# A 32x32 matrix per head, loaded into four groups of partitions: one transfer with a leading stride of 0, or four transfers

## The chip, the cores and the metric

The kernel runs on one core of a Trainium2 chip. The metric is the time of one execution on the device in microseconds, as the median of several runs. TensorE is written PE (its weight loads PEld), VectorE DVE, ScalarE ACT, GpSimd POOL; SP issues all transfers of this kernel.

## The reference

A recurrent attention block and a gated feed-forward block behind it:

```python
# r, k, v, w, a, b: (B, H, S, D) = (4, 8, 768, 40)
for t in range(S):
    y[:, :, t] = einsum('bhd,bhde->bhe', rt, state)
    Sa = einsum('bhde,bhe->bhd', state, at)
    state = state * wt[:, :, None, :] - einsum('bhd,bhe->bhde', Sa, bt)
    state = state + einsum('bhd,bhe->bhde', vt, kt)
x = y.transpose(0, 2, 1, 3).reshape(B * S, H * D)          # 3072 x 320
xn = x / sqrt(mean(x * x) + 1e-6) * rms_g
out = (silu(xn @ w_gate) * (xn @ w_val)) @ w_out           # 320 -> 1536 -> 320
```

The inputs arrive in double precision and are narrowed to fp32 in the kernel for the weights.

## The kernel before, in words

The 768 steps are cut into 24 chunks of 32. Within a chunk the recurrence is solved with matrices, for all 32 pairs of batch and head at once. Each chunk passes three functions:

- `front(c)` loads the tokens (`wan`, `kbn`, `VU`), turns them on TensorE and builds, over five levels, the 32x32 triangular matrix of each pair in the tile `LT`. At its end the lower half of `LT` is written to a buffer in memory, `sB` (32 pairs by 1024 numbers, two transfers), and from there it is loaded into the tile `M` (128 partitions by 32 by 32). `M` holds the 32 matrices four times, once in each group of 32 partitions. There is one `M` buffer.
- `inverse(c)` inverts them by substitution on VectorE, in 31 steps of two operations (`tmp<-Yi,M` and `Yi<-Yi,tmp`). Each group of 32 partitions does 8 of the 32 rows of the inverse (`Yi`), which is why each needs its own copy of `M`. The result goes through the buffer `sY` (four transfers) back into `LT` (two transfers).
- `main(c)` uses the inverse and the state `ST`, computes the outputs `y` of the chunk over the levels (`psC`), turns and normalises them (`ss`, `x`) and puts them into `xg`.

After every second chunk, `feed(g)` runs the feed-forward block on 256 rows: six pairs of weight tiles `wf` (five buffers, loaded again from `sW` each time), into `psH`, `sg`, `hT` and `psO`. Before the first chunk is done, `narrow` prepares the weights in `sW`.

No engine's order is written out by hand. Every operation is added to a `Plan` with its engine, a due time, a cost and its operands. `Plan.issue` then plays the engines in its own time: whichever engine is free takes, of the operations whose inputs it holds to be ready, the one with the earliest due time. The program is issued in that order, and each engine executes its own part strictly in order. The price of a transfer is a term of the plan (line 216 on): 0.06 on the queue, and its result is held to be ready 2.2 us and the bytes at 200 GB/s later, plus 0.1:

```python
    def dma(due, o, i, by="SP"):
        q, t = {"SP": (nc.sync, 0.06), "POOL": (nc.gpsimd, 1.0)}[by]
        n = size(i) * list(i.ap)[0][1]
        plan.add(by, due, t, lambda: q.dma_start(out=o, in_=i), [o], [i], 2.2 + n * 4 / 200e3)
```

`n` counts the elements of the source's access pattern, repeats included. The due time of the transfers at the end of `front(c)` is `(c - 2) * T + T - 8`, that of the inverse steps `(c - 1) * T + 4 + i`, with `T = 46`.

In the profile the helpers' lines stand for whole classes of operations: L183 is any two-operand VectorE operation, L195 the masked copy into `LT`, L219 any transfer, L222 any matmul, L225 any turn. So rows are told apart by the names of their tiles.

Of the kernel before, what the change touches and what calls it, by code (L numbers as in the profile page):

```python
# [17 lines left out]
C = 32  # L18
# [89 lines left out]
def kernel(  # L108
# [42 lines left out]
    BH = B * H  # L151
# [17 lines left out]
    def side(t, l, x):  # L169

        return t.rearrange("p n (g x l) -> p n g x l", x=2, l=l)[:, :, :, x, :]
# [4 lines left out]
    def size(ap):  # L176
        n = 1
        for _, m in list(ap.ap)[1:]:
            n *= m
        return n  # L180

    def tt(due, o, a, b, op):
        plan.add("DVE", due, 0.145 + 0.00104 * size(o), lambda: nc.vector.tensor_tensor(o, a, b, op), [o], [a, b])  # L183
# [10 lines left out]
    def where(due, o, m, a):  # L194
        plan.add("DVE", due, 0.16 + 0.00104 * size(o), lambda: nc.vector.copy_predicated(o, m, a), [o], [m, a, o])  # L195

    def copy(due, o, a):
        plan.add("ACT", due, 0.16 + 0.00083 * size(o), lambda: nc.scalar.copy(o, a), [o], [a])  # L198
# [11 lines left out]
    def ptt(due, o, a, b, op):  # L210
        plan.add("POOL", due, 0.2 + 0.0021 * size(o), lambda: nc.gpsimd.tensor_tensor(o, a, b, op), [o], [a, b])  # L211

    def pcopy(due, o, a):
        plan.add("POOL", due, 0.15 + 0.0014 * size(o), lambda: nc.gpsimd.tensor_copy(o, a), [o], [a])
# [6 lines that stand above are left out]
    def mm(o, lhsT, rhs, start=True, stop=True):  # L221
        return o, lhsT, rhs, lambda: nc.tensor.matmul(o, lhsT, rhs, start=start, stop=stop, skip_group_check=True)  # L222
# [4 lines left out]
    def pe(due, time, steps):  # L227
        def issue():
            for s in steps:
                s[3]()  # L230
        plan.add("PE", due, time, issue, [s[0] for s in steps], [x for s in steps for x in s[1:3]])
# [19 lines left out]
    for p0, kt, src in ((0, 0, 0), (0, 1, P), (0, 2, 2 * P), (64, 2, 2 * P)):  # L251
        m = min(P, DM - src)
# [64 lines left out]
    def turned(due, t, tag):  # L317

        ps = ps_[tag].next().rearrange("p u f -> p (u f)").rearrange("p (n t) -> p n t", n=N)
        pe(due, 0.95, [flip(ps[:, n, :], t[:, n].rearrange("p o e -> p (o e)"), ident) for n in range(N)])  # L320
        return ps

    def tokens(due, t, i, x, src, tk):
        dma(due, flat(t)[rows(i, x), :, 0:D], src[2 * i:2 * i + 2, :, tk, :].rearrange("q h s d -> s (q h) d"))

    def natural(due, l, K):
        ps = turned(due, K.rearrange("p (n i) x s -> p n i (x s)", i=2), "B")
        t = KN_[l].next()
        copy(due, t[:, 0:NI * D].rearrange("p (n o e) -> p n o e", n=N, o=2),
             ps.rearrange("p n (o e) -> p n o e", o=2)[:, :, :, 0:D])  # L330
        return t
# [5 lines left out]
    def front(c):  # L337

        z = Z[c] = {}
        d = (c - 2) * T  # L340
        tk = slice(c * C, (c + 1) * C)
        wa, kb, z["VU"] = wan.next(), kbn.next(), VU_.next()
        for i in range(2):
            tokens(d - T, wa, i, 0, w, tk)
            tokens(d - T, wa, i, 1, a, tk)
            tokens(d - T, kb, i, 0, k, tk)
            tokens(d - T, kb, i, 1, b, tk)
            tokens(d - T, z["VU"], i, 0, v, tk)
        ps = turned(d, wa, "B").rearrange("p n (i x t) -> p (n i) x t", i=2, x=2)
        Tt = T_.next()  # L350
        z["T"] = Tl = {}
        o = 0
        for l in LEVELS + (32,):
            Tl[l] = Tt[:, o:o + NI * C // l].rearrange("p (n t) -> p n t", n=NI)
            o += NI * C // l
        copy(d, Tl[1], ps[:, :, 0, :])
        A = A_.next()
        copy(d, A, ps[:, :, 1, :])
        K = K_.next()
        copy(d + 2, K.rearrange("p (n i) x s -> p n (i x s)", n=N), turned(d + 2, kb, "B"))  # L360
        LT = z["LT"] = LT_.next()
        z["KN"] = {1: flat(kb).rearrange("p a e -> p (a e)")}
        for j, l in enumerate(LEVELS):
            G = C // (2 * l)
            due = d + 5 + 7.5 * j
            gr = ps_["B"].next().rearrange("p o (n t) -> p o n t", n=N)[:, :, :, 0:16]
            pe(due, 0.95, [mm(gr[half(i), o, n, :], K[part(o), 2 * n + i].rearrange("p x s -> p (x s)"),
                              side(A, l, 1)[part(o), 2 * n + i]) for n, i, o in each])
            where(due, side(LT, l, 1), side(msk, l, 1)[:, j:j + 1].bitcast(U32).to_broadcast((P, NI, G, l)),
                  gr.rearrange("p o n t -> p (o n) t").rearrange("p n (g l) -> p n g l", g=G))  # L370
            if l > 1:
                z["KN"][l] = natural(due + 2, l, K)

            t = Tl[l].rearrange("p n (g x) -> p n g x", x=2)
            by = [t[:, :, :, x, None].to_broadcast((P, NI, G, l)) for x in range(2)]
            K1 = K_.next()
            if G == 1 or l == 1:
                lr = lambda t: t.rearrange("p n x (g h l) -> p n x h (g l)", h=2, l=l)
                tt(due, lr(K1)[:, :, :, 0], lr(K)[:, :, :, 0], t[:, :, None, :, 1].to_broadcast((P, NI, 2, 16)), MUL)
            else:  # L380
                for x in range(2):
                    tt(due, side(K1[:, :, x], l, 0), side(K[:, :, x], l, 0), by[1], MUL)
            for x in range(2):
                copy(due, side(K1[:, :, x], l, 1), side(K[:, :, x], l, 1))
            A1 = A_.next() if l < 16 else aP_.next()
            ptt(due, side(A1, l, 1), side(A, l, 1), by[0], MUL)
            pcopy(due, side(A1, l, 0), side(A, l, 0))
            tt(due, Tl[2 * l], t[:, :, :, 0], t[:, :, :, 1], MUL)
            K, A = K1, A1

        due = d + T - 8
        sB = sB_.next()
        for i in range(2):
            dma(due, sB[i * NI:(i + 1) * NI].rearrange("n (s t) -> s n t", s=C), LT[rows(i, 1)])
        z["M"] = M = M_.next()
        dma(due, M.rearrange("p s t -> p (s t)"), bass.AP(sB.tensor, sB.offset, [[0, 4], [C * C, BH], [1, C * C]]))
        z["KN"][32] = natural(due, 32, K)
        z["aP"] = A

# [198 lines left out]
    for c in range(-2, NCH):  # L598
        if c >= 0:
            main(c)  # L600
            if c % CG == CG - 1:
                feed(c // CG)
        if c + 2 < NCH:
            front(c + 2)
            inverse(c + 2)
# [32 lines left out]
```

## Time and profile before

| | |
|---|---|
| time, median of 3 runs | 1665.75 us (1657.48 to 1687.96) |
| the profiled execution's own time | 1676.31 us |
| its span | 1674.5 us |
| mean granted clock of TensorE | 0.884 |
| busy: PE, DVE, ACT, POOL | 82%, 51%, 27%, 12% |
| transfers | 146.19 MB, mean 87 GB/s |
| chain that ended last, by line | PE psH 23%, PE psC 16%, DMA M<-sB 14% |

The span leaves out 1.8 us of the execution's time. Times in the trace count from the span's start. A wait in brackets, `[6.93 <-DMA M<-sB]`, says how long the engine was idle before the instruction and what ended it.

### The profile page before, as it was taken

What the parts mean: (1) busy time and instruction counts of PE and PEld (TensorE: products, weight loads), DVE (VectorE), ACT (ScalarE), POOL (GpSimd) and SP (SyncE); (2) the same over time, 40 slices, a digit from 0 to 9 for tenths busy, and PEclk for the clock granted to TensorE, in tenths of its full rate; (3) what the DMA queues carried; (4) which work ended last, traced back from release to release, by engine and by line L of the source; (5) the groups of instructions that cost most, each with busy time, mean ns of one, the idle gap of its engine ahead of it and who ended that gap; (6) DMA issues with size and microseconds to landing.
All of it is one profiled execution on the core that took longest, in us unless ns stands there. A gap on an engine that the chain in (4) does not pass through costs nothing.

```text
span 1674.5 us, 65373 instructions
## 1 busy us (share of the span) xinstructions
PE 1370.3 (82%) x29632; PEld 1095.6 (65%) x29632; DVE 859.4 (51%) x2767; ACT 444.0 (27%) x805; POOL 202.1 (12%) x360
## 2 busy tenths in 40 slices
PE   4546579889897898888888889879889979879776
PEld 3446577667676676676667667667667767656654
DVE  7766745445455455455445545545645645543211
ACT  2222323223233232232232322223322322311100
POOL 4101210101111111110110110110110110100000
PEclk9997559797998998998998989999989989989878
DMA  7453523342424434433433434443343343333211
GB/s 149 140 137 98 140 41 80 80 89 61 95 66 93 106 67 104 83 74 91 94 75 97 84 76 98 81 84 90 82 88 86 85 95 83 70 80 86 73 48 44
DMA packets 298806, 146.19 MB, mean 87 GB/s; under 512 B 261664, under 2 KB 275488, under 8 KB 298528
## 3 DMA queue, kind: packets, MB, share of 16 engines
q1 hardware_dynamic: 298528, 142.01, 37.6%
q8 instruction: 232, 3.80, 1.0%
q14 instruction: 46, 0.38, 0.1%
HBM read 125.83 MB, written 16.12 MB: 85 GB/s over the span
## 4 chain that ended last, share of the span: by engine, by line
PE 64%; DMA 17%; DVE 8%; issue 5%; ACT 4%; SPq 2%; POOL 0%; DVEq 0%; ACTq 0%; POOLq 0%
PE psH L222 23%; PE psC L222 16%; DMA M<-sB 14%; PE psO L222 9%; PE psB L225 8%; PE psB L222 4%; PE psC L225 4%; SPq L219 2%; DMA sB<-LT 1%; DVE y L183 1%; DVE hT L183 1%; ACT Xs L202 1%; ACT K L198 1%; DMA kbn<-in_b_dram 1%; DVE Yi L183 1%
## 5 line engine op out<-in xcount | busy, mean ns | idle before, releaser
L222 PE MATMUL psH<-xg,wf 128*128 128x256 f32 (+1 forms) x1728 | 425.3, 441 | 70.3 <-DVE xg L183 70.3
L222 PEld LDWEIGHTS psH<-xg,wf 128*128 128x128 f32 (+1 forms) x1728 | 285.6, 210 | 168.3 <-DVE xg L183 71.7
L183 DVE TENSOR_TENSOR tmp<-Yi,M 128x60 f32<-128x60 f32 (+24 forms) x744 | 174.9, 235 | 157.5 <-DMA M<-sB 141.4
L222 PE MATMUL psO<-wf,hT 128*128 128x320 f32 x576 | 202.3, 477 | 22.2 <-DVE hT L183 21.8
L183 DVE TENSOR_TENSOR Yi<-Yi,tmp 128x60 f32<-128x60 f32 (+24 forms) x744 | 189.0, 254 | 17.3
L222 PE MATMUL psB<-A,K 40*64 40x16 f32 x7680 | 150.7, 217 | 36.3 <-ACT K L198 20.7
L222 PEld LDWEIGHTS psB<-A,K 40*64 40x64 f32 x7680 | 139.9, 150 | 61.2 <-issue 30.8
L225 PE MATMUL psB<-ident,K 128*128 128x128 f32 x960 | 153.2, 311 | 27.8 <-DVE LT L195 23.4
L183 DVE TENSOR_TENSOR sg<-psH,sg 128x512 f32<-128x512 f32 x72 | 49.7, 690 | 234.6 <-ACT sg L207 234.6
L198 ACT COPY KN<-psB 128x640 f32<-128x640 f32 x120 | 83.1, 693 | 320.1 <-PE psB L225 312.7
L211 POOL TENSOR_TENSOR A<-A,T 128x256 f32<-128x256 f32 x96 | 72.0, 751 | 720.9 <-ACT A L198 292.9
L225 PEld LDWEIGHTS psB<-ident,K 128*128 128x128 f32 x960 | 125.5, 160 | 37.9 <-DVE LT L195 24.4
L222 PEld LDWEIGHTS psO<-wf,hT 128*128 128x128 f32 x576 | 104.3, 201 | 58.1 <-DVE hT L183 25.3
L222 PEld LDWEIGHTS psC<-As,KN 64*64 64x64 f32 x6144 | 109.4, 147 | 26.1 <-issue 24.6
L222 PE MATMUL psC<-As,KN 64*64 64x16 f32 x6144 | 117.8, 216 | 8.1 <-issue 3.9
L207 ACT ACTIVATE sg<-psH 128x512 f32<-128x512 f32 x72 | 43.0, 597 | 295.9 <-PE psH L222 295.9
L183 DVE TENSOR_TENSOR K<-K,T 128x512 f32<-128x512 f32 (+1 forms) x192 | 99.1, 516 | 29.1 <-PE psB L225 19.9
L183 DVE TENSOR_TENSOR y<-y,psC 128x256 f32<-128x256 f32 (+1 forms) x192 | 57.6, 319 | 109.9 <-PE psC L222 107.6
L198 ACT COPY K<-K 128x256 f32<-128x256 f32 x240 | 88.5, 415 | 85.9 <-DVE K L183 83.6
L195 DVE COPY_PREDICATED LT<-msk,psB 128x256 f32<-128x256 uint32 x120 | 65.8, 549 | 34.8 <-PE psB L222 34.2
L183 DVE TENSOR_TENSOR As<-psC,msk 128x256 f32<-128x256 f32 x120 | 42.0, 417 | 48.6 <-PE psC L222 48.6
L222 PE MATMUL psC<-Xs,LT 32*32 32x40 f32 x1536 | 38.1, 208 | 25.9 <-DMA LT<-sY 15.4
(96 smaller groups left out, 1361.9 us busy)
## 6 DMA issues: line engine op xcount, KB each, us to landing
wf<-sW SPq DMA_DIRECT2D x144, 480.0 KB, 3.8
M<-sB SPq DMA_DIRECT2D x24, 512.0 KB
sW<-hT SPq DMA_DIRECT2D x24, 240.0 KB, 3.7
wan<-in_w_dram SPq DMA_DIRECT2D x48, 80.0 KB, 6.8
wan<-in_a_dram SPq DMA_DIRECT2D x48, 80.0 KB, 3.0
kbn<-in_k_dram SPq DMA_DIRECT2D x48, 80.0 KB, 3.5
kbn<-in_b_dram SPq DMA_DIRECT2D x48, 80.0 KB, 7.7
VU<-in_v_dram SPq DMA_DIRECT2D x48, 80.0 KB, 2.5
```

What stands on the lines that cost most here:

```text
L183: plan.add("DVE", due, 0.145 + 0.00104 * size(o), lambda: nc.vector.tensor_tensor(o, a, b, op), [o], [a, b])
L195: plan.add("DVE", due, 0.16 + 0.00104 * size(o), lambda: nc.vector.copy_predicated(o, m, a), [o], [m, a, o])
L198: plan.add("ACT", due, 0.16 + 0.00083 * size(o), lambda: nc.scalar.copy(o, a), [o], [a])
L202: plan.add("ACT", due, 0.16 + 0.00083 * size(o), lambda: nc.scalar.mul(o, a, by), [o], ins)
L207: plan.add("ACT", due, 0.16 + 0.00083 * size(o), lambda: nc.scalar.activation(o, a, f, **kw), [o] + ([acc] if acc is not None else []), [a])
L211: plan.add("POOL", due, 0.2 + 0.0021 * size(o), lambda: nc.gpsimd.tensor_tensor(o, a, b, op), [o], [a, b])
L219: plan.add(by, due, t, lambda: q.dma_start(out=o, in_=i), [o], [i], 2.2 + n * 4 / 200e3)
L222: return o, lhsT, rhs, lambda: nc.tensor.matmul(o, lhsT, rhs, start=start, stop=stop, skip_group_check=True)
L225: return o, i, ident, lambda: nc.tensor.transpose(o, i, ident)
```

## The change

The transfer into `M` read the 32 rows of `sB` four times, by a leading dimension of 4 with stride 0. Now four transfers read them, each into its 32 partitions.

```diff
         z["M"] = M = M_.next()
-        dma(due, M.rearrange("p s t -> p (s t)"), bass.AP(sB.tensor, sB.offset, [[0, 4], [C * C, BH], [1, C * C]]))
+        for m in range(4):
+            dma(due, M[m * BH:(m + 1) * BH].rearrange("p s t -> p (s t)"), sB)
```

The bytes moved are the same, 512 KB for each chunk. In the plan the parts have prices of their own, and so the order changes on all engines. Three places, at the eleventh and twelfth chunk's load:

SP, at the eleventh load, before. `sY` and `LT<-sY` belong to the inverse of the chunk before; `kbn` and `wan` are tokens of the next.

```order
L219 DMA LT_137<-sY_221 32x16x32 x2
L219 DMA sB_218<-LT_138 32x16x32 x2
L219 DMA wf_212<-sW_72 128x960
L219 DMA M_188<-sB_218 128x1x1024
L219 DMA wf_208<-sW_73 128x960
L219 DMA kbn_121<-in_k_dram 32x16x40
```

And now:

```order
L219 DMA LT_137<-sY_221 32x16x32 x2
L219 DMA sB_218<-LT_138 32x16x32 x2
L219 DMA M_188<-sB_218 32x1024 x4
L219 DMA wf_212<-sW_72 128x960
L219 DMA wf_208<-sW_73 128x960
```

The four parts stand together, in the place of the one, and here ahead of one weight tile that stood ahead of it.

VectorE, at the first step of the eleventh inverse, before. `y_199` is the output of the chunk two before it; the masked copy is the last that writes `LT_138`.

```order
L195 COPY_PREDICATED LT_138<-msk,psB_223 128x16x16
L183 TENSOR_TENSOR y_199<-y_199,T_179 128x32x8
L183 TENSOR_TENSOR y_199<-y_199,psC_222 128x8x2x8 x2
L183 TENSOR_TENSOR y_199<-y_199,T_179 128x64x4
L183 TENSOR_TENSOR y_199<-y_199,psC_222 128x8x4x4 x2
L183 TENSOR_TENSOR y_199<-y_199,T_179 128x128x2
L183 TENSOR_TENSOR y_199<-y_199,psC_222 128x8x8x2 x2
L183 TENSOR_TENSOR tmp_191<-Yi_189,M_188 128x31
L183 TENSOR_TENSOR y_199<-y_199,T_179 128x256
L183 TENSOR_TENSOR Yi_189<-Yi_189,tmp_191 128x31
L183 TENSOR_TENSOR y_199<-y_199,psC_222 128x2x8x16
```

And now:

```order
L195 COPY_PREDICATED LT_138<-msk,psB_223 128x16x16
L183 TENSOR_TENSOR sg_213<-psH_224,sg_213 128x512
L183 TENSOR_TENSOR hT_215<-psH_224,sg_213 128x512
L183 TENSOR_TENSOR tmp_191<-Yi_189,M_188 128x31
L183 TENSOR_TENSOR y_199<-psC_222,T_179 128x2x8x16
L183 TENSOR_TENSOR Yi_189<-Yi_189,tmp_191 128x31
L183 TENSOR_TENSOR y_199<-y_199,psC_222 128x2x8x16
L183 TENSOR_TENSOR tmp_192<-Yi_189,M_188 128x30
L183 TENSOR_TENSOR y_199<-y_199,T_179 128x32x8
```

The first step, which reads `M`, stood ahead of two `y` operations; now it stands ahead of all twelve of them.

VectorE, at the first step of the twelfth inverse, before. The `T` rows belong to the next `front`, `ss` leads to `xg`.

```order
L183 TENSOR_TENSOR y_200<-y_200,psC_222 128x2x8x16
L183 TENSOR_TENSOR T_177<-T_177 128x256
L183 TENSOR_TENSOR T_177<-T_177 128x128
L183 TENSOR_TENSOR T_177<-T_177 128x64
L188 TENSOR_SCALAR ss_202<-ss_202 128x1
L183 TENSOR_TENSOR T_177<-T_177 128x32
L183 TENSOR_TENSOR T_177<-T_177 128x16
L183 TENSOR_TENSOR tmp_192<-Yi_190,M_188 128x31
L183 TENSOR_TENSOR Yi_190<-Yi_190,tmp_192 128x31
```

And now:

```order
L183 TENSOR_TENSOR y_200<-y_200,T_177 128x64x4
L183 TENSOR_TENSOR y_200<-y_200,psC_222 128x8x4x4
L183 TENSOR_TENSOR tmp_192<-Yi_190,M_188 128x31
L183 TENSOR_TENSOR y_200<-y_200,psC_222 128x8x4x4
L183 TENSOR_TENSOR Yi_190<-Yi_190,tmp_192 128x31
L183 TENSOR_TENSOR y_200<-y_200,T_177 128x128x2
L183 TENSOR_TENSOR tmp_191<-Yi_190,M_188 128x30
L183 TENSOR_TENSOR y_200<-y_200,psC_222 128x8x8x2
```

The first step stood behind all of `y`, `T` and `ss`; now it stands ahead of the last six `y` operations and of `T` and `ss`. Over the steady chunks before, the first step stands ahead of 2 and of 0 `y` operations in turn; now ahead of 12, 6, 6, 0, 0 and 4, in a cycle of six.

## The prediction

> **What bounds the kernel now.** I read the page first: its busy times, its slices and its costliest groups.
>
> ```profile
> span 1674.5 us, 65373 instructions
> PE 1370.3 (82%) x29632; PEld 1095.6 (65%) x29632; DVE 859.4 (51%) x2767; ACT 444.0 (27%) x805; POOL 202.1 (12%) x360
> PEclk9997559797998998998998989999989989989878
> L183 DVE TENSOR_TENSOR tmp<-Yi,M 128x60 f32<-128x60 f32 (+24 forms) x744 | 174.9, 235 | 157.5 <-DMA M<-sB 141.4
> ```
>
> TensorE is busy 82% of the span, so what leaves it idle sets the time. VectorE waited 141.4 us for the load of `M`. The share of the steady stage comes from the view by stretches (columns: stretch, its length, busy time and instruction count of PE, PEld, DVE, ACT and POOL, granted clock, DMA share, GB/s).
>
> ```profile
> 480.00:1500.00 1020.00, 883.22 (x20324) 701.32 (x20321) 533.44 (x1765) 291.32 (x529) 124.86 (x226) 0.92 0.40 87
> ```
>
> This stage holds 17 of the 24 loads of `M`. TensorE is idle 1020 − 883 = 137 us in it, 8.0 us for each chunk, and runs at 0.92 of its clock. The waits in the same stretch, first TensorE's, then VectorE's:
>
> ```profile
> PE psH L222 <- DVE xg L183: 69.6, 9, 9.2
> PE psC L222 <- DVE y L183: 31.3, 8, 5.7
> DVE tmp L183 <- DMA M<-sB: 115.6, 17, 9.8
> ```
>
> Two waits make 100.9 of the 137 us: 9 times TensorE waits for `xg`, 8 times for `y`, in turn, and VectorE waits 17 times for `M`. The timeline shows that these are one thing:
>
> ```profile
> 694.43 0.19 DVE L183 TENSOR_TENSOR tmp<-Yi,M 128x31 f32<-128x31 f32 x1 [6.93 <-DMA M<-sB]
> 695.47 1.09 PE L222 MATMUL psC<-ident,y 40*64 40x40 f32 x32 [5.75 <-DVE y L183]
> ...
> 757.07 0.19 DVE L183 TENSOR_TENSOR tmp<-Yi,M 128x31 f32<-128x31 f32 x1 [9.78 <-DMA M<-sB]
> 759.52 4.94 PE L222 MATMUL psH<-xg,wf 128*128 128x256 f32 x12 [9.18 <-DVE xg L183]
> ```
>
> VectorE stops at the first step of the inverse. The last `y` operations, or those that lead to `xg`, stand behind it in its order, and TensorE starves about a microsecond after VectorE is free again. So the load of `M` is on the path in each chunk.
>
> The stall costs a second time, through the clock (the last column but two is the granted clock):
>
> ```profile
> 690.00:696.00 6.00, 0.53 (x20) 0.53 (x24) 1.47 (x8) 0.95 (x2) 0.00 (x0) 0.82 1.03 90
> 696.00:702.00 6.00, 6.00 (x45) 4.39 (x38) 3.85 (x15) 1.77 (x5) 3.05 (x6) 0.61 0.40 59
> ...
> 748.00:754.00 6.00, 1.81 (x67) 1.36 (x67) 0.00 (x0) 1.75 (x4) 2.26 (x5) 0.82 0.70 112
> 754.00:760.00 6.00, 0.48 (x1) 0.48 (x2) 2.75 (x11) 0.74 (x2) 0.00 (x0) 0.50 0.52 126
> 760.00:766.00 6.00, 6.00 (x61) 4.16 (x62) 4.42 (x21) 0.81 (x2) 0.00 (x0) 0.50 0.23 67
> 766.00:772.00 6.00, 6.00 (x163) 4.72 (x158) 0.92 (x3) 1.41 (x3) 0.00 (x0) 0.75 0.01 3
> ```
>
> Taking the clock as either 1 or 0.5, a mean c over 6 us means 12(1 − c) us at half speed. Work done there takes twice its time, so half of the busy part is lost. After the `y` stall: 4.7 us, all busy, and some 0.5 before it, 2.6 lost. After the `xg` stall: 6.0 + 3.0 busy and some 0.5 before, 4.75 lost. The mean is 3.7 us for each chunk, 63 us over the 17.
>
> **The load of M, before and after.** Issue to landing, from the chain that ended last (first and last of its 15 such rows in the stage, together 176.8 us, so 11.8 each), and one load in a quiet place:
>
> ```profile
> 498.60 12.37 DMA M<-sB
> ...
> 1482.47 11.31 DMA M<-sB
> ```
> ```profile
> 294.20 0.56 SPq L219 DMA_DIRECT2D M<-sB  x1
> 304.10 0.19 DVE L183 TENSOR_TENSOR tmp<-Yi,M 128x31 f32<-128x31 f32 x1 [0.45 <-DMA M<-sB]
> ```
> ```profile
> 296.00:298.00 2.00, 2.00 (x49) 1.96 (x46) 0.00 (x0) 0.03 (x1) 0.00 (x0) 0.50 0.23 74
> 298.00:300.00 2.00, 2.00 (x45) 1.67 (x46) 0.00 (x0) 0.69 (x1) 0.00 (x0) 0.50 0.25 68
> ```
>
> With hardly another transfer beside it the load still took 9.9 us: the DMA share is 0.23 to 0.25, the work of 4 of the 16 engines, at some 70 GB/s. Load for load, other transfers do better (columns: operation, count, size, median us from issue to landing):
>
> ```profile
> wf<-sW SPq DMA_DIRECT2D x144, 480.0 KB, 3.8
> kbn<-in_b_dram SPq DMA_DIRECT2D x48, 80.0 KB, 7.7
> wf<-in_moe_w_gate_dram SPq DMA_DIRECT2D x24, 128.0 KB, 2.6
> sB<-LT SPq DMA_DIRECT2D x48, 64.0 KB, 2.0
> ```
>
> The weights bring nearly the volume of `M` in 3.8 us. What limits `M` is therefore the shape of the one transfer (a leading dimension of 4), and parts whose leading dimension is 32 have no such limit. The new load is three more issues and then one part's landing. An issue on SP costs about 0.56 us:
>
> ```profile
> L219 SPq DMA_DIRECT2D M<-sB x24: 559/560/651, 48.4 to 1482.5; - x24
> ```
>
> Low end: 1.7 + 2.0 (as `sB`) = 3.7 us. High end: 1.7 + 7.7 (as the slowest loads that run beside it) = 9.4. A part has the size of the 128 KB load (1.7 + 2.6 = 4.3), and all four together are like the 480 KB load (5.5); I take **5.0**, 6.8 us less than now.
>
> The Trainium skill bears on this twice, in "DMA: Bandwidth & Descriptors", section "Rules for kernel authors". One rule says that a leading zero-stride dimension of c copies confines a transfer to c engines; the share of 0.25 agrees. Another speaks against the change: two transfers to disjoint partition halves are served one after the other, so one 128-partition transfer should be used. If that applied here with full fixed costs, the load would stay near 10 us; this is the rival "no change" below.
>
> **What the planner makes of it.** Its price for the old load is 0.06 + 2.2 + 524,288/200,000 = 4.9 us; for four parts it is 4 × 0.06 + 2.2 + 131,072/200,000 = 3.1, so it puts the first inverse step 1.8 us earlier in its own time. The old wait agrees with the error of the old price: 11.8 − 4.9 = 6.9, against a measured 115.6/17 = 6.8. By the same reckoning the new wait is 5.0 − 3.1 = 1.9 us. The rows of the order show how: the first step now stands ahead of 12 and 6 `y` operations where it stood ahead of 2 and 0. That gives part of the gain back, since a wait there holds more of `y`, and the inverse steps between its rows (0.19 us each) stretch it.
>
> **The sum**, in the profiled execution:
>
> - Idle of TensorE for each chunk: 100.9/17 = 5.9 us at a wait of 6.8, so its queue covers 0.9. At a wait of 1.9 it would be 1.0; for the chunks in which the whole of `y` stands behind the wait I put the mean at 1.4. Saved: 4.5 × 17 = 77 us.
> - Clock: 63 us are at stake. The `y` stalls should become too short to lower the clock; some `xg` stalls stay several us long. I count 60%: 38 us.
> - Before 480 us:
>
> ```profile
> DVE tmp L183 <- DMA M<-sB: 25.8, 6, 6.7
> ```
>
>   Six waits go to about 1.9 each, 14 us, and some 6 for the clock: 20 us.
> - Added: three issues for each chunk, 72 × 0.56 = 40 us of SP's time. SP mostly waits for free weight buffers:
>
> ```profile
> SPq L219 <- PE psO L222: 292.7, 65, 16.1
> ```
>
>   So it is covered; without the cover each of them delays what stands behind it by 1.7 us for each chunk, 40 us in all. Behind `M` stand loads of weights and tokens, and in one place in six the two `LT` transfers that end an inverse. The next reader of that tile comes 25 us after them:
>
> ```profile
> 739.11 1.73 SPq L219 DMA_DIRECT2D LT<-sY  x2
> ...
> 764.39 2.35 PE L222 MATMUL psC<-VU,LT 32*32 32x40 f32 x64
> ```
>
> - The loads of tokens that stood behind `M` on four engines land sooner. No wait in TensorE's list names them, so I count nothing.
>
> Together 77 + 38 + 20 = 135: 1676.3 − 135 = 1541 us for a run like the profiled one. The median of the three runs, 1665.75, lies 0.6% below it, so I predict **1532 us**, 8% less.
>
> **Rivals.**
>
> - *All of it goes.* If the load lands in 3.7 us and TensorE's queue covers the rest, 100 us of idle time, 63 of clock and 30 before 480 go: 1676 − 193 = 1483, on the median's level 1474. For it: 480 KB in 3.8 us. Against it: the early place of the first step. Chance 0.15.
> - *The planner gives it back.* Where the step stands ahead of the whole of `y`, VectorE may wait as long as before and hold more. If the place decides, some 2.5 us for each chunk remain of the gain and no clock: 17 × 2.5 + 15 = 57, so 1619, or 1609. For it: the rows of the order; against: only one place in six is that bad. Chance 0.20.
> - *No change.* The parts are served one after the other, 4 × 2.6 = 10.4 us, and the wait stays near 10.4 − 3.1 = 7.3: 1666. Against it: two `sB` parts issued 679.12 on had both landed at 682.14, 3.0 us for two at 2.0 each. That the transfer doesn't spread gives the same. Chance 0.08.
>
> ```profile
> 679.12 1.55 SPq L219 DMA_DIRECT2D sB<-LT  x2
> ...
> 679.47 2.67 DMA sB<-LT
> ```
>
> - *Slower.* Each part now meets the token loads on all engines. VectorE reaches the step 1.8 us earlier, so from a landing of 6.8 + 3.1 = 9.9 us on, its wait is longer than today's. At 12 us it would be 8.9, 2.1 more over 24 chunks, 50 us: 1716 on the median's level. Against it: the high end above is 9.4. Chance 0.04.
>
> **How the numbers follow.** My forecast has a chance of 0.53; the landing's 3.7 to 9.4 and the shares returned spread it over 1490 to 1580. The range reaches to "all of it" below and to "given back" above: 1465 to 1630. A measurement of this kernel can tell about 2% (33 us) from no change. Faster than 1632: 0.53 + 0.15 + nearly all of 0.20 = 0.87; within 2%: 0.09; slower: 0.04.
>
> **What would show it.** The last part lands 4 to 6 us after the first is issued; VectorE's wait at `tmp` falls from 6.8 us to about 2; TensorE's waits for `xg` and `y` fall from 101 us to some 25; the clock over the steady stage rises from 0.92 to about 0.96. I am wrong if the parts land in turn, or if the wait at `tmp` stays above 4 us although the load is short.

## The result, and the profile after

| | before | after |
|---|---|---|
| median of six runs | 1666.42 us | 1599.11 us |
| lowest to highest | 1655.28 to 1687.96 | 1594.55 to 1615.9 |
| profiled execution, its span | 1676.31, 1674.5 | 1605.55, 1603.8 |

The ratio is 0.9625, with a 95% interval of 0.9561 to 0.969: 3.75% faster, where 8% was forecast. The time lies in the range, near the rival "the planner gives it back" (1609), but the gain went another way than that rival says.

The page of the changed kernel first: span, busy times, granted clock by slices, the chain that ended last by engine, the group that waited for `M`, and three rows of the loads (count, size, median us from issue to landing).

```profile
span 1603.8 us, 65497 instructions
...
PE 1384.5 (86%) x29632; PEld 1110.6 (69%) x29632; DVE 854.5 (53%) x2767; ACT 441.6 (28%) x805; POOL 206.1 (13%) x360
...
PEclk9999979798999799798999789989989779799878
...
PE 71%; DVE 8%; issue 6%; DMA 6%; ACT 5%; SPq 3%; POOL 1%; DVEq 0%; POOLq 0%; ACTq 0%
...
L183 DVE TENSOR_TENSOR tmp<-Yi,M 128x60 f32<-128x60 f32 (+24 forms) x744 | 179.5, 241 | 98.8 <-DMA M<-sB 83.7
...
M<-sB SPq DMA_DIRECT2D x96, 128.0 KB, 3.5
...
wan<-in_w_dram SPq DMA_DIRECT2D x48, 80.0 KB, 3.1
...
kbn<-in_b_dram SPq DMA_DIRECT2D x48, 80.0 KB, 3.2
```

The wait for `M` fell from 141.4 to 83.7 us, and each part of the load lands in 3.5. TensorE is busy for 14 us more than before with the same 29,632 matmuls: they ran slower, where the forecast had them run faster. The account below shows that this is where the missing part of the forecast gain went.

One load of the changed kernel in the timeline: the four issues, and the first step that waits for them. Below it the row of the same load in the chain that ended last.

```profile
640.45 1.71 SPq L219 DMA_DIRECT2D M<-sB  x4
...
645.38 0.19 DVE L183 TENSOR_TENSOR tmp<-Yi,M 128x31 f32<-128x31 f32 x1 [4.61 <-DMA M<-sB]
```
```profile
641.27 3.52 DMA M<-sB
```

From the first issue it takes 4.3 us to the landing in the chain (641.27 + 3.52), and 4.9 to the first step; 5.0 was forecast. Over the 16 chunks of the account below, first issue to first step takes 5.2 us on the mean, 4.2 to 6; in the kernel before, the same measure is 11.8.

The account compares the same work, cut from each kernel: the 16 chunks from the eighth to the twenty-fourth first step of an inverse. The views by stretches (columns as in the prediction), of before and then of after:

```profile
511.10:1493.90 982.80, 855.20 (x19680) 679.46 (x19680) 517.88 (x1708) 283.91 (x515) 120.37 (x217) 0.92 0.40 87
```
```profile
475.50:1430.00 954.50, 886.61 (x19712) 708.62 (x19712) 514.99 (x1706) 283.07 (x516) 126.74 (x222) 0.89 0.38 89
```

TensorE's idle time (length less busy) fell from 127.6 to 67.9 us, but its clock fell from 0.92 to 0.89. The waits in the stretch after, VectorE's for `M` and TensorE's:

```profile
DVE tmp L183 <- DMA M<-sB: 64.4, 16, 5.9
```
```profile
PE psC L225 <- ACT x L202: 14.9, 6, 4.0
PE psB L225 <- DMA kbn<-in_b_dram: 14.3, 8, 3.5
...
PE psC L222 <- DVE y L183: 3.6, 2, 2.2
PE psC L222 <- DVE xg L183: 3.5, 3, 1.3
```

VectorE still waits 4.0 us for each load, but TensorE's waits for `xg` and `y`, 94.5 us in the stretch of before, are down to 7. Waits for `x` (6.7 us before) and `kbn` stand in their place.

The clock records show two levels, full and half speed. With them the period of a chunk is its idle time, plus its work at full speed, plus half of the busy time at half speed. From the trace's matmul and clock records, us for each of the 16 chunks:

| kernel | period | idle | at half speed | of that busy | work at full speed |
|---|---|---|---|---|---|
| before | 61.43 | 7.98 | 10.01 | 6.40 | 50.25 |
| after | 59.66 | 4.25 | 12.80 | 11.87 | 49.48 |
| first experiment below (old order, four parts) | 56.33 | 3.03 | 6.61 | 6.25 | 50.17 |

So of the 70.7 us that the span lost, the 16 chunks gave 28: 60 from idle time and 12 from matmuls counted a little shorter, less 44 from the clock. Before the eighth step 36 us went, and behind the last 7.

### The profile page after: what moved, and what is told of

It reads as the page before. It is cut to its first block, busy times and chain, and to the rows that moved or that the text cites. A ratio compares the mean times of both kernels' runs of the same rounds, so it can differ in the third digit from the quotient of the medians.

```text
span 1603.8 us, 65497 instructions
## 1 busy us (share of the span) xinstructions
PE 1384.5 (86%) x29632; PEld 1110.6 (69%) x29632; DVE 854.5 (53%) x2767; ACT 441.6 (28%) x805; POOL 206.1 (13%) x360
## 4 chain that ended last, share of the span: by engine, by line
PE 71%; DVE 8%; issue 6%; DMA 6%; ACT 5%; SPq 3%; POOL 1%; DVEq 0%; POOLq 0%; ACTq 0%
PE psH L222 22%; PE psC L222 17%; PE psO L222 11%; PE psB L225 9%; PE psB L222 7%; PE psC L225 5%; SPq L219 3%; DMA kbn<-in_b_dram 2%; DMA M<-sB 2%; ACT Xs L202 1%; DVE hT L183 1%; DVE y L183 1%; DMA sB<-LT 1%; ACT K L198 1%; DVE tmp L183 1%
## 5 line engine op out<-in xcount | busy, mean ns | idle before, releaser
L222 PE MATMUL psH<-xg,wf 128*128 128x256 f32 (+1 forms) x1728 | 411.8, 430 | 2.0 <-DVE xg L183 1.4
L222 PEld LDWEIGHTS psH<-xg,wf 128*128 128x128 f32 (+1 forms) x1728 | 278.3, 205 | 95.8 <-issue 55.4
L183 DVE TENSOR_TENSOR tmp<-Yi,M 128x60 f32<-128x60 f32 (+24 forms) x744 | 179.5, 241 | 98.8 <-DMA M<-sB 83.7
L222 PE MATMUL psO<-wf,hT 128*128 128x320 f32 x576 | 209.2, 490 | 19.1 <-DVE hT L183 18.3
L222 PEld LDWEIGHTS psB<-A,K 40*64 40x64 f32 x7680 | 154.9, 163 | 62.0 <-issue 30.0
L222 PE MATMUL psB<-A,K 40*64 40x16 f32 x7680 | 165.7, 226 | 32.2 <-ACT K L198 18.4
L183 DVE TENSOR_TENSOR Yi<-Yi,tmp 128x60 f32<-128x60 f32 (+24 forms) x744 | 177.3, 238 | 15.6
L183 DVE TENSOR_TENSOR y<-y,psC 128x256 f32<-128x256 f32 (+1 forms) x192 | 58.8, 318 | 67.9 <-PE psC L222 66.3
L225 PE MATMUL psB<-ident,kbn 128*128 128x128 f32 x192 | 37.1, 357 | 27.2 <-DMA kbn<-in_b_dram 21.3
```

What stands on the lines that cost most here:

```text
L225: return o, i, ident, lambda: nc.tensor.transpose(o, i, ident)
```

## The experiments

All ratios are to the kernel before on the same chip, with their 95% intervals.

### Order and transfer apart

The change does two things: four parts in place of one, and by the parts' lower prices another order of every engine's work. The first kernel issues the four parts in one piece of the plan at the old price, so every engine keeps the order of before.

```diff
-        for m in range(4):
-            dma(due, M[m * BH:(m + 1) * BH].rearrange("p s t -> p (s t)"), sB)
+        def load(M=M, sB=sB):
+            for m in range(4):
+                nc.sync.dma_start(out=M[m * BH:(m + 1) * BH].rearrange("p s t -> p (s t)"), in_=sB)
+        plan.add("SP", due, 0.06, load, [M.rearrange("p s t -> p (s t)")], [sB], 2.2 + 4 * C * C * BH * 4 / 200e3)
```

> Four transfers, but planned as one piece at the old price (0.06 on the queue, ready 4.8 us later), so that every engine keeps the order of before. Theory 1 (the new order gives the gain back: the first inverse step stands ahead of y, and TensorE comes to its small matmuls at half clock): VectorE's wait at tmp falls from 6.8 us to about 1, TensorE's idle time from 8.0 to about 3 us for each chunk, the half-speed time from 10 to 4 us, 1530 to 1560 us. Theory 2 (the clock falls in these stages whatever the order, once a short gap comes before the small matmuls): idle falls the same, but half-speed time stays at 10 to 13 us for each chunk, 1585 to 1605 us.

The second has the order of the changed kernel with the one old transfer: four pieces are planned, of which the last issues the whole (`whole` is the old source with its leading stride of 0).

```diff
         for m in range(4):
-            dma(due, M[m * BH:(m + 1) * BH].rearrange("p s t -> p (s t)"), sB)
+            def load(M=M, whole=whole, last=m == 3):
+                if last:
+                    nc.sync.dma_start(out=M.rearrange("p s t -> p (s t)"), in_=whole)
+            plan.add("SP", due, 0.06, load, [M[m * BH:(m + 1) * BH].rearrange("p s t -> p (s t)")], [sB],
+                     2.2 + C * C * BH * 4 / 200e3)
```

> One transfer with the leading stride of 0, planned at the prices of the four, so that every engine has the order of the changed kernel and the load still takes some 11.8 us. If the order alone matters for the clock (theory 1), it is slower than before: the wait at tmp grows from 6.8 to about 9 to 10 us, 1700 to 1740 us. If the order is neutral, the wait is longer but holds nothing more: 1660 to 1690 us.

| | old order | new order |
|---|---|---|
| one transfer | 1 | 1.0452 (1.0379 to 1.0525), 1747.0 us |
| four parts | 0.9304 (0.9234 to 0.9375), 1553.55 us | 0.9625 (0.9561 to 0.969), 1599.11 us |

The transfer is worth 7 points (hundredths of the time before) in the old order and 8 in the new. The new order costs 3 to 4.5; with the one transfer it is slower than the range of 1700 to 1740 us that was expected. Their stretches of 16 chunks, the first kernel's and the second's, each followed by its waits in that stretch:

```profile
483.20:1384.50 901.30, 852.75 (x19709) 677.98 (x19701) 519.53 (x1708) 283.25 (x515) 121.53 (x218) 0.94 0.41 94
```
```profile
DVE tmp L183 <- DMA M<-sB: 16.4, 9, 2.9
...
PE psH L222 <- DVE xg L183: 11.9, 7, 2.6
```
```profile
504.00:1565.90 1061.90, 913.76 (x19712) 728.63 (x19712) 516.38 (x1707) 283.52 (x516) 128.23 (x222) 0.85 0.36 80
```
```profile
DVE tmp L183 <- DMA M<-sB: 170.2, 17, 13.5
```

At like numbers of matmuls TensorE is busy 852.75 us in the old order and 886.61 (above) in the new; 855.20 and 913.76 with one transfer. So the new order costs 34 us of busy time, or 59: it costs clock. It costs idle time as well, some 20 us in either pair (48.5 against 67.9, and 127.6 against 148.1).

### Is it the wait for M?

The changed kernel's order and the old one, each with the inverse's steps reading a constant tile instead of `M`, which is still loaded. The plan still counts `M` as an input, so every order stays, but on the chip nothing waits for the load any more.

```diff
-            tt(d + i, tmp, Y[:, 0:n, i:i + 1].to_broadcast((P, n, m)), M[:, i:i + 1, i + 1:].to_broadcast((P, n, m)), MUL)
+            def first(tmp=tmp, y=Y[:, 0:n, i:i + 1].to_broadcast((P, n, m)),
+                      c=eye[:, 7:8, i + 1:].to_broadcast((P, n, m))):
+                nc.vector.tensor_tensor(tmp, y, c, MUL)
+            plan.add("DVE", d + i, 0.145 + 0.00104 * size(tmp), first, [tmp],
+                     [Y[:, 0:n, i:i + 1].to_broadcast((P, n, m)), M[:, i:i + 1, i + 1:].to_broadcast((P, n, m))])
```

> The changed kernel with every engine's order as it is, but the inverse steps read a constant tile of the same shape in place of M (so the inverse is not that of the reference); M is still loaded by four transfers. VectorE then never waits for M. If the wait at tmp is what the new order costs (wait theory), the time falls from 1599 to that of the old order, 1545 to 1565 us, and the half-speed time from 12.8 to about 7 us for each chunk. If the new order costs it by itself (where the dense matmuls stand among the small ones, interleaved y), it stays at 1585 to 1605 us.

> The same constant tile in the old order with four transfers. In the old order VectorE hardly waits for M any more, so both theories expect 1545 to 1556 us; what is below the old order's 1553.55 is the price of the waits that are left there.

New order 1574.4 us, 0.9393 (0.9319 to 0.9467); old order 1528.73, 0.9114 (0.9029 to 0.9199). What is left of the wait is worth 2.3 points in the new order and 1.9 in the old. The order costs 2.8 points with no wait for `M` at all. The new order's time lies between the two that were expected (1545 to 1565 if the wait is what it costs, 1585 to 1605 if not), the old order's below its 1545 to 1556. The stretches, new order and then old:

```profile
466.56:1388.46 921.90, 866.24 (x19627) 692.49 (x19626) 516.80 (x1708) 284.78 (x519) 127.72 (x223) 0.92 0.41 92
```
```profile
481.50:1360.76 879.26, 843.66 (x19752) 671.49 (x19752) 523.28 (x1708) 285.68 (x519) 123.32 (x222) 0.96 0.42 97
```

Taking the rest of the wait away also brought clock back: TensorE is busy for 20 us less than in the changed kernel, and for 9 less in the old order. So a stall does cost clock. But even the old order with no wait has 4.7 us at half speed in each chunk: part of the slow clock never came from the load. And between these two orders the new one still has 20 us more idle and 23 more busy.

### Is it the wait for kbn?

In the new order the transposes of `kbn` wait for its load (14.3 us above). Two kernels let these transposes read a constant, one with `M` as in the changed kernel, one with the constant for `M` too; `kbn` is still loaded.

```diff
-        copy(d + 2, K.rearrange("p (n i) x s -> p n (i x s)", n=N), turned(d + 2, kb, "B"))
+        pk = ps_["B"].next().rearrange("p u f -> p (u f)").rearrange("p (n t) -> p n t", n=N)
+        pe(d + 2, 0.95, [(pk[:, n, :], kb[:, n].rearrange("p o e -> p (o e)"), ident,
+                          lambda q=pk[:, n, :]: nc.tensor.transpose(q, ident, ident)) for n in range(N)])
+        copy(d + 2, K.rearrange("p (n i) x s -> p n (i x s)", n=N), pk)
```

> The changed kernel, every order as it is, but the turn of the tokens kbn at the start of a chunk reads a constant tile in place of kbn (the values are not those of the reference); kbn is still loaded. TensorE's waits for the kbn loads (14.3 us in the steady stage of the changed kernel) then go. If these late loads are the new order's price, the half-speed time falls as well, since most long half-speed stretches begin at such a wait: 1560 to 1575 us, where the changed kernel takes 1599. If they are one gap of several, only their own length goes: 1583 to 1592 us.

> Both constants in the new order: no wait for M and none for kbn. If waits (for M and kbn) are all that the new order costs, this comes to the old order without the wait for M, a ratio to before of 0.911 or 1515 to 1535 us, with some 4.7 us of half-speed time for each chunk. If the order itself keeps the clock low (long stretches of small matmuls behind a gap, dense ones late), it stays at a ratio of 0.925 to 0.94 with 7 us or more of half-speed time.

Without the wait for `kbn`: 1609.26 us, 0.9611 (0.9515 to 0.9707), no gain over the changed kernel; both expectations (1560 to 1575, 1583 to 1592) missed. Without both: 1554.39, 0.929 (0.9199 to 0.9382), against 0.9114 for the old order without the wait for `M`. Its stretch:

```profile
463.44:1369.18 905.74, 856.55 (x19627) 683.48 (x19626) 517.61 (x1708) 285.38 (x519) 128.76 (x223) 0.93 0.41 94
```

With neither wait some 2 points of the order's cost remain, though the two intervals just touch. Against the old order without the wait for `M`, half of this is idle time (49.2 us against 35.6) and half is clock (busy 856.55 us against 843.66; 7.9 us at half speed in each chunk against 4.7).

### What lowers the clock

Trains of the kernel's matmuls by themselves, and none of its other work: dense ones (128x128 by 256 columns) and small ones (32x32 by 40, and 40x64 by 16), behind pauses of 1.5, 3 and 8 us.

```
for f, n in ((lt, 18), (ak, 24)):
    rest(8); dense(50); f(n)
    rest(1.5); f(n)
    rest(8); f(n)
    dense(40)
rest(8); dense(50)
rest(1.5); dense(50)
rest(3); dense(50)
```

> No part of the computation; zeros are written. Trains of matmuls of three shapes of the kernel (128x128 with 256 columns: dense; 32x32 with 40 columns, as VU,LT; 40x64 with 16 columns, as A,K), after pauses of about 1.5, 3 and 8 us or directly after dense ones. If the clock follows pauses alone, it falls in each pause of 8 us, not at 1.5, and comes back within about 7 us of any train. If it follows how much of the array works, it falls within the small trains without any pause, and comes back only in dense ones. Theory 2 needs something between: a short pause before a small train lowers it, and the small train does not bring it back.

Stretches with the pauses of 1.5 and 3 us between dense trains, a train of the 32x32 ones with the dense train behind it, and a train of the 40x64 ones (columns: stretch, length, busy PE, PEld, DVE, POOL, granted clock, DMA share, GB/s):

```profile
510.00:520.00 10.00, 8.24 (x39) 6.94 (x38) 2.50 (x7) 0.00 (x0) 1.00 0.01 2
560.00:570.00 10.00, 6.79 (x31) 5.64 (x31) 3.88 (x9) 0.00 (x0) 1.00 0.00 0
...
160.00:196.00 36.00, 36.00 (x1088) 36.00 (x1085) 0.00 (x0) 0.00 (x0) 0.50 0.01 4
200.00:210.00 10.00, 10.00 (x46) 8.71 (x46) 0.00 (x0) 0.00 (x0) 0.97 0.00 0
...
390.00:410.00 20.00, 20.00 (x760) 20.00 (x756) 0.00 (x0) 0.00 (x0) 0.50 0.02 5
```

The pause of 3 us between dense trains lowers nothing here; it lies across two steps of the grid that is told of below. Small matmuls keep TensorE busy for 36.00 of 36 us, and 20.00 of 20, and stay at half speed; dense ones bring the clock back. In the Trainium skill, "TensorE: Matmul & The Clock Gate", section "Part 1: The HAM clock gate (the "warmup" mystery)", the full clock comes after about 3.4 us of sustained busy time. The dense trains agree with it; the 36.00 us of small ones do not, so there the measurement decides.

Then mixtures: k dense matmuls to s groups of eight small ones (40x64 by 16), first behind a pause of 8 us, then directly behind dense ones.

```
for k, s, n in ((1, 12, 14), (2, 9, 14), (3, 6, 16), (4, 4, 18), (5, 2, 20)):
    rest(8); mixed(k, s, n)
    rest(0.5); dense(50); mixed(k, s, n)
```

> No part of the computation; zeros are written. Mixed trains of dense matmuls (128x128, 256 columns) and groups of 8 small ones (40x64, 16 columns) in the ratios 1 to 12, 2 to 9, 3 to 6, 4 to 4 and 5 to 2, each once after a pause of 8 us (at half speed) and once directly behind dense ones (at full speed). If dense work brings the clock back and small work doesn't hold it, there is a share of dense work below which the train falls from full speed and never comes back, and above which it comes back within 7 us; I expect it between 2 to 9 and 4 to 4.

```profile
35.00:115.00 80.00, 80.00 (x2410) 71.04 (x2410) 0.35 (x2) 0.00 (x0) 0.50 0.02 4
405.00:465.00 60.00, 60.00 (x1482) 51.31 (x1481) 0.00 (x0) 0.00 (x0) 0.50 0.01 3
480.00:495.00 15.00, 15.00 (x304) 12.34 (x303) 0.00 (x0) 0.00 (x0) 0.50 0.01 3
500.00:560.00 60.00, 59.14 (x1329) 50.82 (x1328) 1.90 (x6) 0.00 (x0) 1.00 0.01 3
580.00:620.00 40.00, 40.00 (x1332) 33.83 (x1330) 0.00 (x0) 0.00 (x0) 1.00 0.02 4
```

The rows are 1:12 behind a pause, 2:9 behind dense ones, 3:6 behind a pause, early and late (the late row has dense ones at its end), and 3:6 behind dense ones. The first two never come back to full speed by themselves; 3:6 does so 20 us after its start, 4:4 and 5:2 after 8 to 9 us (7 at most were expected). Directly behind dense ones the same 3:6 stays at full speed. How much TensorE does counts, not how long it is busy.

**The rule that the traces give.** The clock records of each run change only on a grid of 3.41 us. For each step of the grid I summed the columns that TensorE streamed, each matmul record with its columns times its active rows / 128, and looked at the clock of the next step. Ten kernels of this case (before, after, six experiments above, and two below on the price, 7.5 and 3.0), 480 to 1380 us:

| columns in a step | steps | next step at full speed |
|---|---|---|
| under 1400 | 327 | 0 |
| 1400 to 1600 | 116 | 15 |
| 1600 to 1800 | 122 | 100 |
| 1800 to 2000 | 168 | 154 |
| over 2000 | 1905 | 1905 |

A limit at 1600 tells 2587 of the 2638 steps (98%); "as in the step before" tells 2220, and the best limit on the share of a step in which TensorE is busy some 2360. The weight is less sure: with the used columns of the array counted too, the best limit tells some 2580. In the two kernels of trains it tells 171 of 172 and 276 of 277 (a dense train at full speed has about 4000). At half speed the same train does half as much in a step. So work between 1600 and 3200 keeps a full clock and also keeps a half one: by this rule a single poor step costs as long as no dense step follows.

So it matters what the order puts behind a gap. Two falls serve as examples. First one of the long falls of the changed kernel: TensorE's timeline, then the steps of the grid.

```profile
892.42 2.52 PE L222 MATMUL psH<-xg,wf 128*128 128x256 f32 x12
896.13 0.66 PE L225 MATMUL psC<-ident,x 128*128 128x128 f32 x3 [1.18 <-ACT x L202]
897.09 1.82 PE L225 MATMUL psB<-ident,kbn 128*128 128x128 f32 x8 [0.30 <-DMA wan<-in_w_dram]
900.18 2.35 PE L222 MATMUL psC<-VU,LT 32*32 32x40 f32 x64 [1.27 <-DVE xg L183]
902.46 1.91 PE L222 MATMUL psB<-A,K 40*64 40x16 f32 x64
```
```profile
893.89:897.30 3.41, 1.92 (x11) 0.87 (x11) 3.03 (x17) 1.75 (x4) 1.00 (x3) 1.00 1.07 188
897.30:900.71 3.41, 2.13 (x24) 1.73 (x23) 3.41 (x9) 1.97 (x4) 2.20 (x4) 0.50 0.14 19
900.71:904.13 3.42, 3.42 (x120) 3.33 (x114) 1.57 (x6) 0.03 (x1) 0.00 (x0) 0.50 0.00 0
```

The columns in the steps from 893.89 on are 1488, 1032, 816, 1843, 894 and 1528 (to some 100, by how a matmul across a border is shared out): a few short waits, then mostly small matmuls, and the clock is back only at 914.37, after five steps at half speed. The limit does not tell two of these six: behind 1843 the clock stayed at half, and behind 1528 it came back. In the old order with four parts, a worse stall:

```profile
711.08 4.94 PE L222 MATMUL psH<-xg,wf 128*128 128x256 f32 x12 [2.35 <-DVE xg L183]
```
```profile
709.70:713.11 3.41, 2.03 (x5) 1.68 (x6) 3.34 (x12) 1.57 (x4) 0.21 (x1) 0.50 1.00 226
713.11:716.53 3.42, 3.42 (x27) 1.94 (x27) 2.93 (x14) 0.00 (x0) 0.00 (x0) 0.50 0.16 42
716.53:719.94 3.41, 3.41 (x66) 2.64 (x61) 0.00 (x0) 0.00 (x0) 0.00 (x0) 1.00 0.00 0
```

965 columns from 706.29, then 997, then 1667: the dense `psH` stands right behind the wait, and the fall ends after two steps. Over the 16 chunks, falls and their length in steps:

| kernel | falls | of 1 or 2 steps | longest | steps at half speed |
|---|---|---|---|---|
| before | 21 | 12 | 5 | 47 |
| after | 23 | 15 | 6 | 60 |
| old order, four parts | 24 | 24 | 2 | 31 |
| new order, one transfer | 28 | 12 | 8 | 92 |

### The price

With four parts in one piece, the price alone sets the order. 7.5, 4.4 and 3.0 us in place of the old 4.8 (all without the 0.06 for an issue):

```diff
+        plan.add("SP", due, 0.06, load, [M.rearrange("p s t -> p (s t)")], [sB], 7.5)
```

> Four transfers planned as one piece that is ready 7.5 us later, so that the first inverse step stands later in VectorE's order than before. Theory 1: the wait at tmp is near 0 and nothing of y or xg stands behind it: as the old order or better, 1520 to 1555 us. Theory 2: idle as low, half-speed time still 10 us or more for each chunk, 1580 to 1600 us.

> Four transfers planned as one piece that is ready 4.4 us after its issue (old price 4.8, new 2.9 for each part). The first inverse step stands ahead of 3 and 0 y operations in turn (old order 2 and 0; new order 12, 6, 6, 0, 0, 4). Wait theory: as the old order, 1545 to 1570 us. If small changes of the order move the time at random, as the price of 7.5 did (1616 us), anything from 1550 to 1620.

> Four transfers planned as one piece that is ready 3.0 us after its issue: the first inverse step stands ahead of 6 y operations in every chunk. Wait theory: VectorE waits some 3 to 5 us at tmp in each chunk with half of y behind it, 1585 to 1615 us. If only the places with the whole of y behind the step cost much, 1560 to 1575 us.

> The version with the price of 4.4 again, in five rounds, as the candidate for the best one: a ratio to before of 0.915 to 0.93 if its first result holds; above 0.935 it would be no better than the old order at the old price (0.930).

| price | 3.0 | four times 2.9 (the change) | 4.4 | 4.8 (the old) | 7.5 |
|---|---|---|---|---|---|
| ratio | 0.9544 | 0.9625 | 0.9213, again 0.9177 | 0.9304 | 0.9663 |
| interval | 0.9463 to 0.9625 | 0.9561 to 0.969 | 0.9137 to 0.9289, 0.9129 to 0.9225 | 0.9234 to 0.9375 | 0.9607 to 0.972 |

At 7.5 VectorE waits 0.6 us for `M` in all, but in this order TensorE waits for `kbn` instead. Its 1616.4 us lie outside both expected ranges (1520 to 1555, 1580 to 1600); how the later step brings this wait about is open:

```profile
PE psB L225 <- DMA kbn<-in_b_dram: 48.0, 15, 3.9
```

The best prices, 4.4 and 4.8, are those nearest to the measured 5.2 us from issue to first step; between 4.8 and 7.5 nothing was tried. The version at 4.4 is the fastest that computes the whole block: 1547.77 us over six runs, against 1683.98 for before on that chip. It beats before by 8% and the changed kernel by 4 to 5 points. Against the old price it is about a point faster in each of two measurements, and in the first the intervals overlap.

## Why the prediction was right or wrong

**Right.** *The landing:* 5.0 us forecast, 5.2 measured on the mean to the first step (4.9 in the load shown, of which the landing is 4.3). The parts do not land in turn: the rival "no change" had 10.4 us for them. That the shape of the one transfer was the limit, and not the volume, is shown by the pair in one order: the same 512 KB in four parts cut 7% from the time. How many engines each part used was not measured. *The added issues* cost nothing that shows; SP's issue of a part takes less than that of the whole:

```profile
L219 SPq DMA_DIRECT2D M<-sB x96: 312/419/1033, 48.2 to 1425.4; - x96
```

*The token loads* do land sooner, two of them (`kbn` from `b` 3.2 us instead of 7.7, `wan` from `w` 3.1 instead of 6.8); whether anything came of it was not measured. *Idle time:* 4.5 us for each chunk forecast, 3.7 measured in the new order and 4.95 in the old (79 us over 16 chunks, against 77 over 17).

**Wrong: the clock term**, "63 us are at stake. I count 60%: 38 us". With it the clock of the stage was to rise from 0.92 to about 0.96; it fell to 0.89. The stake was about right: 6.40 us busy at half speed for each chunk is 3.2 lost, 51 us over 16. But none of it came back. In the old order the half-speed time fell from 10.0 to 6.6 us a chunk, and nearly all of that had been idle; the busy part went from 6.40 to 6.25, 1 us in all. In the new order it rose to 11.87, so the term is −44 in place of +38, and this 82 us is more than the whole miss of 64. The step that failed is the inference that the stall is what keeps the clock low, and that without the long stalls it stays up. It stands on two stalls that I looked at. The runs show in its place that 24 falls remain in the old order without long stalls, that the weighted work in each 3.41 us tells the clock of the next, and that the order itself costs clock. The forecast saw the order change but priced it at 0.4 us of idle time for each chunk (1.4 in place of 1.0) and at nothing in clock; with four parts it costs 53 us over the 16 chunks, 34 of clock and 19 idle.

**Wrong in size: the wait at `tmp`.** 1.9 us forecast, 4.0 measured. The step that failed is "landing less price". It held roughly for the old order (6.9 against 6.8; with four parts, 5.2 less 4.9, 0.3 against 1.0), but not for the new one (5.2 less 3.1, 2.1 against 4.0); why VectorE comes so early there is open. By the sentence "I am wrong if the wait at `tmp` stays above 4 us although the load is short" it stood right at that mark. TensorE's waits for `xg` and `y` fell to 7 us all the same, further than the 25 forecast. What was left of the wait cost 2.3 points, more of it through the clock than as idle time (20 and 12 us).

**Before the steady stage.** 20 us forecast before 480 us. Up to the eighth first step, at 511 us, there is one chunk more, some 7 us by the forecast (115/17): 27, and 36 were measured; 28 in the old order.

**The rival "the planner gives it back"** has the right time by another account. It had 2.5 us of idle time saved for each chunk and the clock unchanged; measured, 3.7 were saved and the clock got worse. That the new order gives gain back is shown (0.9304 against 0.9625); that most of this goes through the clock is shown by TensorE's busy time in the same work (34 of 53 us). That poor steps make the clock fall is the regularity of ten traces and two kernels of trains. No experiment here moved one group of matmuls alone within the kernel, so which swap of the order costs how much is open.

## What to carry to other kernels

A transfer that reads one source several times through a leading stride of 0 may be far slower than its parts (here 11.8 us against 5.2): compare its landing and the DMA share with a plain load of the same size. Where a planner orders the work by prices, change the transfer and the price apart, and try prices near what the trace measures. Here 4.4 and 4.8 for some 5 us were the best of those tried, worth 3 to 4.5% of the time against the price of the change. When a stall goes, look not only at the gap but at what the matmul engine runs behind it: in the trains here small matmuls kept the clock low, and dense ones restored it.

## What the runs showed of the hardware

The granted clock moves on a grid of 3.41 us, and its next step follows the work of the last one: at full speed behind 2159 of the 2195 steps with over 1600 weighted columns, behind 15 of the 443 with fewer. TensorE busy for 36.00 of 36 us with 32x32 matmuls, or 20.00 of 20 with 40x64 ones, is granted half speed. The 512 KB load of `M` took 9.9 us as one transfer with a leading stride of 0 in a quiet place, 11.8 on the mean, and 5.2 as four parts, each from the first issue to the step that reads it. Two of the 80 KB loads beside it went from 7.7 and 6.8 to 3.2 and 3.1.
